# Value products in one piece and transposes two banks at a time, in a fused attention and two-layer MLP kernel

## Chip, cores and metric

The kernel runs on one core of a Trainium2 chip. The metric is the device time of one execution in microseconds (us); a median is taken over several executions.

## What is computed

The reference takes `q`, `k`, `v` of 4 batches, 8 heads, 576 positions and 64 dimensions. Attention is a sum of two parts: one over means of four neighbouring positions (144 by 144), repeated four times, and one over the seven positions nearest to each query. Its output, 2304 tokens by 512, goes through two MLPs.

```python
def _attn_ref(q, k, v):
    ...
    out_d = sm_attn(q_d, k_d, v_d)
    out_up = np.repeat(out_d, factor, axis=2)
    mask = np.abs(pos[:, None] - pos[None, :]) < factor
    ...
    out_local = np.matmul(attn, v)
    return (out_up + out_local).astype(np.float32)

def _moe_ref(x, w_in, w_out):
    h = x @ w_in
    g = h * (1.0 / (1.0 + np.exp(-1.702 * h)))
    return g @ w_out

def _moe2_ref(x, w1, w2, w3, w_out):
    return ((x @ w1) * (x @ w2) @ w3) @ w_out
```

## The kernel before, in words

The heads are worked on in 16 pairs (`HP` = 4 pairs for each of 4 batches), two heads side by side on the 128 partitions. TensorE is also given the MLPs: every large product is three matmuls of split operands (`mm3`, lines 117 to 120), the rows of L118, L119 and L120.

The program has these stages. First the product `w3 @ w_out2` is made (`w34_mm`, 192 large matmuls), and batch 0 of the attention is mixed into it. Then come five blocks of tokens of the first MLP (`h_step`, `y_step`); in block 0 batch 1 of the attention is mixed in, in block 1 batch 2, in block 2 batch 3. Blocks 3 and 4 and the second MLP (`ab_step`, `o_tile`) have no attention beside them.

The mixing is done by a list of pieces. `stage(n, what, own_exp)` returns the pieces of pair `n`: "T" transposes q and k (`t_piece`; by TensorE for batches 0 and 1 only, by VectorE for the others), "S" the scores (`s_local` twice, `s_pool`), "P" transposes the probabilities (`p_piece`, four transposes a bank), "V" the value products. `att_pieces` puts them into one list for a batch, in which `None` is an empty place, and `Pump` takes one place off the list after each group of three large matmuls (in the blocks after each second group). So a piece of the list is where its TensorE instructions are put among the large matmuls. A scheduler then orders all instructions by the priority that this program order gives and by when it takes them to be ready, so that a piece may come some places later than in the list, or next to another.

Before, "V" has three pieces: `v_pool` (line 404; four products with the pooled values into a PSUM bank `ps_vp`, copied by ScalarE to `od`, line 413), and `v_local` twice (line 415; ten and eight windows of 64 queries into a bank `ps_v`; VectorE adds `od` and writes `xo`, line 426, which SyncE's queue sends to `x_d`, line 430). Each product is recorded as two matmuls, so the rows show 8, 20 and 16. All of `ps_t`, `ps_s`, `ps_sp`, `ps_pt`, `ps_vp` and `ps_v` take turns in the two banks of the pool `pst`. For the four pairs of batch 3 (`LOCAL`) the near positions are not worked out by TensorE but by VectorE and GpSimd from about block 0 on (`l_scores`, `l_values`, the names `prod` and `ql`), and only the pooled part goes through "S", "P" and "V".

The first piece of "P" also calls `v_means` (line 298): GpSimd makes the pooled values `vd` from `s_v`, and ScalarE's queue then issues the load of the next pair's `s_v` (line 256), which has to wait until `vd` is made, as `s_v` has one buffer.

Of the kernel before, what the change touches and what calls it, by code (L numbers as in the profile page):

```python
# [8 lines left out]
F32 = mybir.dt.float32  # L9
# [11 lines left out]
def fused_kernel(ctx, tc, q, k, v, w_in, w_out1, w1, w2, w3, w_out2, out):  # L21
    nc = tc.nc
    B, H, S, D = q.shape
    FAC = 4
    SD = S // FAC
# [7 lines left out]
    HP = H // 2  # L33
    UC = SD // 2
    QB = 64
    NQB = S // QB
# [4 lines left out]
    HQ = (NQB + 1) // 2  # L41
# [3 lines left out]
    LOCAL = {12: 2, 13: 2, 14: 3, 15: 3}  # L45
# [9 lines left out]
    NB = 512  # L55
# [14 lines left out]
    g2p = ctx.enter_context(tc.tile_pool(name="g2p", bufs=2))  # L70
# [6 lines left out]
    pst = ctx.enter_context(tc.tile_pool(name="pst", bufs=2, space=PSUM))  # L77
# [149 lines left out]
    at = {}  # L227

    def head_ap(src, b, hp, tok, dims):
        off = ((b * H + 2 * hp) * S + tok) * D  # L230
        return bass.AP(src.tensor, src.offset + off, dims)
# [28 lines left out]
    def att_load_v(n):  # L260
        b, hp = divmod(n, HP)
        for t, i0, i1 in ((0, 0, HQ), (1, HQ, NQB)):
            vw = at["vw", n, t] = att.tile([KW, i1 - i0, 2, D], F32, tag=f"vw{t}", name="vw")
            for j0, j1 in ((i0, i0 + 1 - t), (i0 + 1 - t, i1 - t), (i1 - t, i1)):
                tok = min(max(j0 * QB - FAC, 0), S - KW)
                if j1 - j0 == 1:
                    nc.sync.dma_start(
                        out=vw[:, j0 - i0], in_=head_ap(v, b, hp, tok, [[D, KW], [S * D, 2], [1, D]]))
                elif j1 > j0:
                    for h in range(2):  # L270
                        nc.sync.dma_start(out=vw[:, j0 - i0:j1 - i0, h], in_=head_ap(
                            v, b, hp, h * S + tok, [[D, KW], [QB * D, j1 - j0], [1, D]]))

    def t_piece(n, name, c):
        if c == 0:
            at[name, n] = att.tile([128, SD, FAC], F32, tag=name + "T", name=name + "T")
        st, dst = at["s" + name, n], at[name, n]
        if n // HP >= PE_T:
            if c == 0:
                nc.vector.transpose(dst.rearrange("p u r -> p (u r)"), st.rearrange("p a b -> p (a b)"))  # L280
        else:
            ps = pst.tile([128, FAC, UC], F32, tag="t", name="ps_t")
            for r in range(FAC):
                nc.tensor.transpose(ps[:, r], st[:, c, r].rearrange("p h d -> p (h d)"), ident[:UC, :UC])
            nc.scalar.activation(dst[:, c * UC:(c + 1) * UC].rearrange("p u r -> p r u"), ps, AF.Copy)
        if c == 1:
            if name == "q":
                d = qd[:, :SD]
            else:
                d = at["kd", n] = att.tile([128, SD], F32, tag="kd", name="kd")  # L290
            if n // HP in QK_V:
                nc.vector.tensor_reduce(d, dst, op=ALU.add, axis=X)
            else:
                nc.gpsimd.tensor_tensor(d, dst[:, :, 0], dst[:, :, 1], op=ALU.add)
                for r in range(2, FAC):
                    nc.gpsimd.tensor_tensor(d, d, dst[:, :, r], op=ALU.add)
# [83 lines left out]
    NPT = NQB + 2 * NPB  # L380
    NPH = 8

    def p_piece(n, i0, i1):
        if i0 % NPH == 0 and i0 // NPH >= (n in LOCAL):
            at["PT", n, i0 // NPH] = att.tile(
                [KW, min(NPH, NPT - i0), 128], F32, tag=f"PT{i0 // NPH}", name="PT")
        i0 = i0 if n not in LOCAL else max(i0, NQB)
        ps = pst.tile([KW, i1 - i0, 128], F32, tag="t", name="ps_pt")
        for i in range(i0, i1):
            if i < NQB:  # L390
                src = at["el", n][:, i]
            else:
                kc, j = divmod(i - NQB, NPB)
                src = at["ep", n][:, j, kc * UC:(kc + 1) * UC]
            nc.tensor.transpose(ps[:, i - i0], src, ident)  # L395
        nc.scalar.activation(at["PT", n, i0 // NPH][:, i0 % NPH:i0 % NPH + i1 - i0], ps, AF.Copy)
        first = i0 == (0 if n not in LOCAL else NQB)
        if first:
            v_means(n)
            if n % HP < HP - 1 and n + 2 < B * HP:  # L400
                att_load(n + 2, "qk")

    def v_pool(n):
        PT, vd = at["PT", n, 1], at["vd", n]
        ps = pst.tile([128, SD], F32, tag="t", name="ps_vp")
        for kc in range(2):
            for h in range(2):
                p = slice(h * D, (h + 1) * D)
                i = NQB + kc * NPB - NPH
                nc.tensor.matmul(  # L410
                    ps[p], vd[:, h, kc], PT[:, i:i + NPB, h * QB:h * QB + PB], start=kc == 0, stop=kc == 1)
        at["od", n] = od = att.tile([128, SD], F32, tag="od", name="od")
        nc.scalar.activation(od, ps, AF.Copy, scale=1.0 / FAC)

    def v_local(n, i0, i1):
        vw, od = at["vw", n, i0 // HQ], at["od", n]
        xo = g2p.tile([128, NB], F32, tag="ys", name="xo")[:, :(i1 - i0) * QB]
        ps = pst.tile([128, (i1 - i0) * QB], F32, tag="t", name="ps_v")
        for i in range(i0, i1):
            for h in range(2):  # L420
                p = slice(h * D, (h + 1) * D)
                nc.tensor.matmul(
                    ps[p, (i - i0) * QB:(i - i0 + 1) * QB], vw[:, i - i0, h], at["PT", n, i // NPH][:, i % NPH, h * QB:(h + 1) * QB],
                    start=True, stop=True)
        u0, u1 = i0 * UB, i1 * UB
        nc.vector.tensor_tensor(
            xo.rearrange("p (u r) -> p u r", r=FAC), ps.rearrange("p (u r) -> p u r", r=FAC),
            od[:, u0:u1].unsqueeze(2).to_broadcast([128, u1 - u0, FAC]), op=ALU.add)
        b, hp = divmod(n, HP)
        nc.sync.dma_start(out=x_d[:, hp, b * S + i0 * QB:b * S + i1 * QB], in_=xo)  # L430
        if i1 == NQB and n + 1 < B * HP and n + 1 not in LOCAL:
            att_load_v(n + 1)


    def l_load(n):
# [57 lines left out]
    def l_out(n, i0, i1):  # L493

        o_d, od = at["od_", n], at["od", n]
        c0, c1 = i0 * QB // 32, i1 * QB // 32
        st = dp.tile([128, c1 - c0, 32], F32, tag="dec", name="ost")
        for i in range(4):
            h, dh = divmod(i, 2)
            nc.sync.dma_start(  # L500
                out=st[i * 32:(i + 1) * 32],
                in_=o_d[h, c0 * 32:c1 * 32, dh * 32:(dh + 1) * 32].rearrange("(c t) d -> t c d", t=32))
        xo = g2p.tile([128, NB], F32, tag="ys", name="xo")[:, :(i1 - i0) * QB]
        nc.vector.transpose(xo, st.rearrange("p c d -> p (c d)"))
        u0, u1 = i0 * UB, i1 * UB
        xv = xo.rearrange("p (u r) -> p u r", r=FAC)
        nc.vector.tensor_tensor(
            xv, xv, od[:, u0:u1].unsqueeze(2).to_broadcast([128, u1 - u0, FAC]), op=ALU.add)
        b, hp = divmod(n, HP)
        nc.sync.dma_start(out=x_d[:, hp, b * S + i0 * QB:b * S + i1 * QB], in_=xo)  # L510

    def stage(n, what, own_exp):
        if what == "T":
            return [lambda name=name, c=c: t_piece(n, name, c) for name in "qk" for c in range(2)]
        if n in LOCAL and what in "SPV":
            if what == "S":
                return [lambda: s_pool(n, False)]
            if what == "P":
                return [lambda: p_piece(n, NPH, NPH + 4), lambda: p_piece(n, NPH + 4, NPT)]
            return [lambda: v_pool(n), lambda: l_out(n, 0, HQ), lambda: l_out(n, HQ, NQB)]  # L520
        if what == "S":
            return [lambda: s_local(n, 0, HQ, own_exp), lambda: s_local(n, HQ, NQB, own_exp), lambda: s_pool(n, own_exp)]
        if what == "P":
            return [lambda i=i: p_piece(n, i, min(i + 4, NPT)) for i in range(0, NPT, 4)]
        return [lambda: v_pool(n), lambda: v_local(n, 0, HQ), lambda: v_local(n, HQ, NQB)]

    def att_pieces(b, own_exp, rest):

# [253 lines left out]
    if True:  # L782
# [72 lines left out]
        local, wait = local_pieces(), [0]  # L855
# [16 lines left out]
        for j in range(nblk):  # L872
# [14 lines left out]
            for f in range(NF):  # L887
# [6 lines left out]
                else:  # L894
# [8 lines left out]
                    if last and f >= NF2 + 2:  # L903
                        for _ in range(2):
                            if w34_raw:
                                fw, t = w34_raw.pop(0)
# [79 lines left out]
```

## Time and profile before

| | us |
|---|---|
| median of 3 runs | 899.37 |
| lowest and highest | 895.59, 905.09 |
| the profiled execution | 903.21 |
| its span on the core | 901.4 |
| mean granted clock of TensorE | 0.936 |

The span holds everything from the first instruction to the last; 1.8 us of the profiled execution lie outside it. A matmul's row ends only when its result is written, while the next one has long begun, so that what a matmul takes of TensorE's time is read from start to start.

### The profile page before, as it was taken

To read this page: it belongs to the slowest core of one execution; us is meant where nothing else is said; L and a number is where in the kernel's file an instruction comes from. 1 tells how busy PE (TensorE), PEld (TensorE's weight loads), DVE (VectorE), ACT (ScalarE), POOL (GpSimd) and SP (SyncE) were. 2 spreads that over 40 slices of the span, in tenths; PEclk is the share of its full clock that TensorE was granted. 3 is DMA by queue.
4 is the path that set the end of the run, shared out by engine and by line. 5 is a ranking of instruction groups with operands and counts; after the bars stand their busy time and mean duration, and the time that the engine had idled before them with its cause. 6 is when DMAs were issued, how large, how long until landed. Compare 5 with 4: busy or idle time off the path is not lost.

```text
span 901.4 us, 13594 instructions
## 1 busy us (share of the span) xinstructions
PE 849.8 (94%) x5132; PEld 712.6 (79%) x5132; DVE 605.9 (67%) x1061; ACT 384.2 (43%) x748; POOL 151.5 (17%) x153
## 2 busy tenths in 40 slices
PE   4788979989899999999999999999999999999998
PEld 3566767767677767767788988888999899989996
DVE  5997588879999999964448784342555554555551
ACT  4667567657654344344436554342212321131111
POOL 7535242134333332310100000000000000000000
PEclk9789888999999999989999999999999999999999
DMA  8875584555563344342357999201646364645521
GB/s 226 281 213 151 158 248 139 154 180 174 133 184 78 84 103 112 96 115 58 67 147 265 330 343 367 84 1 47 245 164 249 136 227 181 227 158 203 206 83 70
DMA packets 140598, 150.76 MB, mean 167 GB/s; under 512 B 86898, under 2 KB 121460, under 8 KB 136436
## 3 DMA queue, kind: packets, MB, share of 16 engines
q1 hardware_dynamic: 119424, 141.21, 48.3%
q10 hardware_dynamic: 21108, 8.69, 4.1%
q8 instruction: 40, 0.66, 0.3%
q14 instruction: 26, 0.21, 0.1%
HBM read 117.75 MB, written 32.11 MB: 166 GB/s over the span
## 4 chain that ended last, share of the span: by engine, by line
PE 69%; DVE 15%; DMA 5%; issue 4%; ACT 3%; POOL 3%; ACTq 0%; SPq 0%; DVEq 0%; POOLq 0%
PE ps_ab L120 6%; PE ps_ab L118 6%; PE ps_ab L119 6%; PE ps_h L118 5%; PE ps_y L118 5%; PE ps_h L119 5%; PE ps_h L120 5%; PE ps_y L120 5%; PE ps_y L119 5%; PE ps_o L119 4%; PE ps_o L120 4%; PE ps_o L118 4%; DVE dec L179 2%; PE ps_pt L395 2%; DVE st L176 2%
## 5 line engine op out<-in xcount | busy, mean ns | idle before, releaser
L118 PE MATMUL ps_h<-x_t,w 128*128 128x512 f32 (+1 forms) x320 | 123.3, 388 | 3.9 <-DVE w L115 2.9
L119 PE MATMUL ps_h<-x_t,w 128*128 128x512 f32 (+1 forms) x320 | 120.4, 376 | 4.1 <-DVE x_t L115 4.1
L118 PE MATMUL ps_y<-gh,w 128*128 128x512 f32 (+1 forms) x320 | 121.6, 381 | 0.0
L120 PE MATMUL ps_h<-x_t,w 128*128 128x512 f32 (+1 forms) x320 | 119.2, 373 | 0.0
L120 PE MATMUL ps_y<-gh,w 128*128 128x512 f32 (+1 forms) x320 | 118.8, 371 | 0.0
L119 PE MATMUL ps_y<-gl,w 128*128 128x512 f32 (+1 forms) x320 | 118.4, 370 | 0.4 <-DVE gl L115 0.4
L120 PE MATMUL ps_ab<-b_t,a_in 128*128 128x384 f32 x336 | 112.5, 335 | 0.0
L118 PE MATMUL ps_ab<-b_t,a_in 128*128 128x384 f32 x336 | 112.5, 335 | 0.0
L119 PE MATMUL ps_ab<-b_t,a_in 128*128 128x384 f32 x336 | 112.4, 334 | 0.0
L115 DVE TENSOR_TENSOR gl<-g_t,gh 128x512 fp32r<-128x512 f32 (+1 forms) x80 | 56.1, 704 | 69.8 <-ACT gh L114 68.8
L624 ACT ACTIVATE g_t<-ps_h 128x512 f32<-128x512 f32 (+1 forms) x80 | 44.0, 553 | 115.1 <-PE ps_h L120 111.5
L118 PEld LDWEIGHTS ps_h<-x_t,w 128*128 128x128 f32 x320 | 60.5, 191 | 18.6 <-DVE w L115 4.6
L119 PEld LDWEIGHTS ps_h<-x_t,w 128*128 128x128 f32 x320 | 61.1, 191 | 14.7 <-DVE x_t L115 5.7
L114 ACT ACTIVATE abh<-ab 128x384 fp32r<-128x384 f32 x24 | 12.6, 526 | 137.2 <-DVE ab L749 137.2
L118 PEld LDWEIGHTS ps_y<-gh,w 128*128 128x128 f32 x320 | 60.3, 189 | 11.8 <-issue 2.3
L120 PEld LDWEIGHTS ps_h<-x_t,w 128*128 128x128 f32 x320 | 61.1, 191 | 10.4 <-issue 0.2
L120 PEld LDWEIGHTS ps_y<-gh,w 128*128 128x128 f32 x320 | 60.4, 189 | 10.4
L119 PEld LDWEIGHTS ps_y<-gl,w 128*128 128x128 f32 x320 | 60.5, 189 | 9.5 <-DVE gl L115 1.0
L118 PEld LDWEIGHTS ps_ab<-b_t,a_in 128*128 128x128 f32 x336 | 63.1, 188 | 0.9
L119 PEld LDWEIGHTS ps_ab<-b_t,a_in 128*128 128x128 f32 x336 | 63.1, 188 | 0.9
L120 PEld LDWEIGHTS ps_ab<-b_t,a_in 128*128 128x128 f32 x336 | 63.1, 188 | 0.0
L179 DVE SCALAR_TENSOR_TENSOR dec<-dec,st 128x512 int32<-128x512 int32 x72 | 58.9, 828 | 5.6 <-ACT dec L166 4.7
(149 smaller groups left out, 1653.1 us busy)
## 6 DMA issues: line engine op xcount, KB each, us to landing
a_in<-a_d SPq DMA_DIRECT2D x24, 1792.0 KB
st<-in_moe_w_dram SPq DMA_DIRECT2D x32, 512.0 KB
a_d<-ap SPq DMA_DIRECT2D x8, 1792.0 KB
st<-in_moe_w_out_dram SPq DMA_DIRECT2D x24, 512.0 KB
st<-in_moe_w_in_dram SPq DMA_DIRECT2D x16, 512.0 KB
yr<-y_d SPq DMA_DIRECT2D x12, 384.0 KB
out_dram<-osb SPq DMA_DIRECT2D x17, 256.0 KB
s_v<-in_v_dram ACTq DMA_DIRECT2D x15, 288.0 KB
```

The costliest lines, as they stand in the source:

```text
L114: nc.scalar.activation(hi, raw, AF.Copy)
L115: lo_eng.tensor_tensor(lo, raw, f32(hi), op=ALU.subtract)
L118: nc.tensor.matmul(ps, ll, rh, start=start, stop=False, skip_group_check=more)
L119: nc.tensor.matmul(ps, lh, rl, start=False, stop=False, skip_group_check=more)
L120: nc.tensor.matmul(ps, lh, rh, start=False, stop=stop, skip_group_check=more)
L176: nc.vector.scalar_tensor_tensor(low, st[:, :, 1], -0x80000000, low, op0=ALU.bitwise_and, op1=ALU.bitwise_or)
L179: nc.vector.scalar_tensor_tensor(t, t, 3, st[:, :, 0], op0=ALU.logical_shift_left, op1=ALU.bitwise_or)
L395: nc.tensor.transpose(ps[:, i - i0], src, ident)
L624: nc.scalar.activation(g[:, :n], ps[:, :n], AF.Gelu_apprx_sigmoid)
```

## The change

"V" becomes one piece at the third of its three places. It takes both banks of `pst` at once: the first holds the pooled products and the last four windows, the second the first five. All TensorE instructions of the pair are written one after the other, then ScalarE's `od`, then VectorE's two `xo`. "T" writes the transposes of both banks of q (and of k) at the place of the second, and "P" those of two banks at the place of the second. The number of places in the list stays the same. No matmul, addition or transfer is added or left out. For batch 3 "V" stays in three pieces.

```diff
-    def v_pool(n):
+    def v_all(n):
+        both = pst.tile([128, NB], F32, tag="t", name="ps_v")
+        rest = pst.tile([128, NB], F32, tag="t", name="ps_v")
+        local = ((HQ, NQB, both[:, SD:SD + (NQB - HQ) * QB]), (0, HQ, rest[:, :HQ * QB]))
+        v_pool_mm(n, both[:, :SD])
+        for i0, i1, ps in local:
+            v_local_mm(n, i0, i1, ps)
+        v_pool(n, both[:, :SD])
+        for i0, i1, ps in local:
+            v_local(n, i0, i1, ps)
+        if n + 1 < B * HP and n + 1 not in LOCAL:
+            att_load_v(n + 1)
...
+        def together(*fns):
+            return [None] * (len(fns) - 1) + [lambda: [fn() for fn in fns]]
+
         if what == "T":
-            return [lambda name=name, c=c: t_piece(n, name, c) for name in "qk" for c in range(2)]
+            return [p for name in "qk" for p in together(*(
+                lambda name=name, c=c: t_piece(n, name, c) for c in range(2)))]
...
         if what == "P":
-            return [lambda i=i: p_piece(n, i, min(i + 4, NPT)) for i in range(0, NPT, 4)]
-        return [lambda: v_pool(n), lambda: v_local(n, 0, HQ), lambda: v_local(n, HQ, NQB)]
+            return [p for i in range(0, NPT, NPH) for p in together(*(
+                lambda i=i: p_piece(n, i, min(i + 4, NPT)) for i in range(i, min(i + NPH, NPT), 4)))]
+        return [None, None, lambda: v_all(n)]
```

**TensorE, the value products of the second pair of batch 2 in block 1.** Before, three groups stand apart (`ps_vp` is the pooled part, `ps_v` the windows, `ps_y` and `ps_h` the MLP):

```order
L410 MATMUL ps_vp<-PT,vd 64x144 x4
L118 MATMUL ps_y<-gh,w 128x512
L119 MATMUL ps_y<-gl,w 128x512
L120 MATMUL ps_y<-gh,w 128x512
...
L422 MATMUL ps_v<-PT,vw 64x64 x10
L118 MATMUL ps_h<-x_t,w 128x512
L119 MATMUL ps_h<-x_t,w 128x512
L120 MATMUL ps_h<-x_t,w 128x512
...
L422 MATMUL ps_v<-PT,vw 64x64 x8
```

In the changed kernel there:

```order
L118 MATMUL ps_h<-x_t,w 128x512
L119 MATMUL ps_h<-x_t,w 128x512
L120 MATMUL ps_h<-x_t,w 128x512
L428 MATMUL ps_v<-PT,vd 64x144 x4
L440 MATMUL ps_v<-PT,vw 64x64 x18
L118 MATMUL ps_h<-x_t,w 128x512
L119 MATMUL ps_h<-x_t,w 128x512
```

All 22 products stand in one row at the place of the last group. Over the 12 pairs of batches 0 to 2, the value products stand in 33 rows without a large matmul between them before, and in 18 now: six pairs in one, six in two. All small products together stand in 140 such rows before, in 111 now.

**ScalarE, the eviction of the pooled products of the second pair of batch 1.** Before (`od` is that eviction, `s_v` the load for the pair after next):

```order
L624 ACTIVATE g_t<-ps_h 128x512
L114 ACTIVATE gh<-g_t 128x512
L413 ACTIVATE od<-ps_vp 128x144
L256 DMA s_v<-in_v_dram 72x4x256
L364 ACT_TABLE_LOAD
```

In the changed kernel:

```order
L114 ACTIVATE w<-dec 128x512 x2
L256 DMA s_v<-in_v_dram 72x4x256
L433 ACTIVATE od<-ps_v 128x144
L366 ACT_TABLE_LOAD
```

The load now stands ahead of `od`; so it does for three of the 12 pairs. On VectorE the two additions of that pair, before and now:

```order
L426 TENSOR_TENSOR xo<-ps_v,od 128x320
L367 TENSOR_REDUCE sm<-ep 128x3
L176 SCALAR_TENSOR_TENSOR st<-st 128x512
...
L426 TENSOR_TENSOR xo<-ps_v,od 128x256
```

```order
L115 TENSOR_TENSOR w<-dec,w 128x512
L448 TENSOR_TENSOR xo<-ps_v,od 128x256
L448 TENSOR_TENSOR xo<-ps_v,od 128x320
L115 TENSOR_TENSOR gl<-g_t,gh 128x512
```

They stood nine rows apart, and now follow one another.

## Rows read from the trace of the kernel before

**Rows 1.** The page, busy time of each engine (share of the span) and instructions.

```profile
PE 849.8 (94%) x5132; PEld 712.6 (79%) x5132; DVE 605.9 (67%) x1061; ACT 384.2 (43%) x748; POOL 151.5 (17%) x153
```

**Rows 2.** Busy time in blocks 0 and 1: stretch, length, engines, clock, DMA share, GB/s.

```profile
198.50:400.00 201.50, 191.15 (x1321) 144.57 (x1320) 186.64 (x300) 100.30 (x162) 66.79 (x48) 0.94 0.48 125
```

**Rows 3.** Waits of TensorE, 56 to 400 us: total us, times, longest us.

```profile
PE ps_pt L395 <- POOL el L375: 5.2, 4, 2.5
...
PE ps_pt L395 <- ACT PT L396: 2.1, 2, 1.3
PE ps_t L284 <- DVE xo L426: 1.7, 1, 1.7
PE ps_v L422 <- ACT od L413: 1.6, 1, 1.6
```

**Rows 4.** Timeline of TensorE, one pair in block 0: start, us, row.

```profile
251.80 0.39 PE L120 MATMUL ps_y<-gh,w 128*128 128x512 f32 x1
252.12 0.72 PE L410 MATMUL ps_vp<-PT,vd 72*64 72x144 f32 x8
252.77 0.50 PE L118 MATMUL ps_y<-gh,w 128*128 128x512 f32 x1
253.10 0.40 PE L119 MATMUL ps_y<-gl,w 128*128 128x512 f32 x1
...
254.03 0.40 PE L120 MATMUL ps_y<-gh,w 128*128 128x512 f32 x1
254.36 1.27 PE L422 MATMUL ps_v<-PT,vw 72*64 72x64 f32 x36
255.56 0.50 PE L118 MATMUL ps_y<-gh,w 128*128 128x512 f32 x1
255.89 0.39 PE L119 MATMUL ps_y<-gl,w 128*128 128x512 f32 x1
```

**Rows 5.** Timeline of TensorE, ten windows alone.

```profile
107.29 0.39 PE L118 MATMUL ps_w<-w,w3t 128*128 128x512 f32 x1
107.61 0.80 PE L422 MATMUL ps_v<-PT,vw 72*64 72x64 f32 x20
108.34 0.50 PE L119 MATMUL ps_w<-w,w3t 128*128 128x512 f32 x1
108.68 0.39 PE L120 MATMUL ps_w<-w,w3t 128*128 128x512 f32 x1
```

**Rows 6.** Timeline of TensorE, pooled products and ten windows without a gap.

```profile
115.91 0.40 PE L119 MATMUL ps_w<-w,w3t 128*128 128x512 f32 x1
116.24 0.73 PE L410 MATMUL ps_vp<-PT,vd 72*64 72x144 f32 x8
116.80 0.75 PE L422 MATMUL ps_v<-PT,vw 72*64 72x64 f32 x20
117.48 0.49 PE L120 MATMUL ps_w<-w,w3t 128*128 128x512 f32 x1
117.91 0.69 PE L422 MATMUL ps_v<-PT,vw 72*64 72x64 f32 x16
```

**Rows 7.** Timeline of TensorE, the end of a bank of transposes of probabilities.

```profile
316.55 0.50 PE L395 MATMUL ps_pt<-ident,ep 128*72 128x128 f32 x3
316.80 0.48 PE L118 MATMUL ps_y<-gh,w 128*128 128x512 f32 x1
317.12 0.40 PE L119 MATMUL ps_y<-gl,w 128*128 128x512 f32 x1
317.35 0.40 PE L120 MATMUL ps_y<-gh,w 128*128 128x512 f32 x1
```

**Rows 8.** Timeline of ScalarE, at the second and the third pair of batch 1.

```profile
207.90 0.29 ACT L413 ACTIVATE od<-ps_vp 128x144 f32<-128x144 f32 x1
...
209.05 1.28 ACT L364 ACT_TABLE_LOAD   x1 [0.85 <-POOL vd L303]
...
237.64 1.28 ACT L364 ACT_TABLE_LOAD   x1 [3.35 <-POOL vd L303]
```

More of the change, by code (lines that the diff above doesn't have):

```diff
@@ L401, in p_piece, with v_far, v_pool_mm @@
                 att_load(n + 2, "qk")
-    def v_pool(n):
+    def v_all(n):
[10 more added lines that the diff above has]
+            att_load_v(n + 1)
+    def v_far(n):
+        ps = pst.tile([128, SD], F32, tag="t", name="ps_vp")
+        v_pool_mm(n, ps)
+        v_pool(n, ps)
+    def v_pool_mm(n, ps):
         PT, vd = at["PT", n, 1], at["vd", n]
-        ps = pst.tile([128, SD], F32, tag="t", name="ps_vp")
         for kc in range(2):
@@ L411, in v_pool, with v_local_mm @@
                     ps[p], vd[:, h, kc], PT[:, i:i + NPB, h * QB:h * QB + PB], start=kc == 0, stop=kc == 1)
+    def v_pool(n, ps):
         at["od", n] = od = att.tile([128, SD], F32, tag="od", name="od")
         nc.scalar.activation(od, ps, AF.Copy, scale=1.0 / FAC)
[L415 to L418, printed above, removed]
+    def v_local_mm(n, i0, i1, ps):
+        vw = at["vw", n, i0 // HQ]
         for i in range(i0, i1):
@@ L424, in v_local @@
                     start=True, stop=True)
+    def v_local(n, i0, i1, ps):
+        od = at["od", n]
+        xo = g2p.tile([128, NB], F32, tag="ys", name="xo")[:, :(i1 - i0) * QB]
         u0, u1 = i0 * UB, i1 * UB
@@ L430, in v_local @@
         nc.sync.dma_start(out=x_d[:, hp, b * S + i0 * QB:b * S + i1 * QB], in_=xo)
-        if i1 == NQB and n + 1 < B * HP and n + 1 not in LOCAL:
-            att_load_v(n + 1)
     def l_load(n):
@@ L518, in stage @@
             if what == "P":
-                return [lambda: p_piece(n, NPH, NPH + 4), lambda: p_piece(n, NPH + 4, NPT)]
-            return [lambda: v_pool(n), lambda: l_out(n, 0, HQ), lambda: l_out(n, HQ, NQB)]
+                return together(lambda: p_piece(n, NPH, NPH + 4), lambda: p_piece(n, NPH + 4, NPT))
+            return [lambda: v_far(n), lambda: l_out(n, 0, HQ), lambda: l_out(n, HQ, NQB)]
         if what == "S":
```

## The prediction

> **What bounds the kernel now.** I read the page's busy times first. TensorE is busy for 849.8 us, 94% of the span, VectorE for 67%, ScalarE for 43% [rows 1]. So the kernel is a stream of matmuls, and what takes TensorE less time, at a place where TensorE sets the pace, comes off the end. Second is the stretch from 198.5 to 400 us, where batches 1 and 2 of the attention are mixed into blocks 0 and 1 and where two thirds of the changed value products stand. There TensorE is busy for 191.15 of 201.5 us, but VectorE for 186.64, which leaves it 14.9 us of idle time [rows 2]. TensorE is still ahead as the bound, by little: what stops VectorE there is soon felt. Third are TensorE's own waits from 56 to 400 us. Four of them are at pieces that the change touches: transposes that wait for GpSimd's normalised `el` (5.2 us in 4), transposes that wait for a bank which ScalarE empties (2.1 us in 2), one that waits for a bank which VectorE's `xo` empties (1.7), and windows that wait for a bank until `od` is copied (1.6) [rows 3]. Last is TensorE's timeline, from start to start, for what one piece among the large matmuls costs.
>
> **What a piece costs.** A large matmul starts 0.23 us after the one before it (317.12 to 317.35 [rows 7]). A piece's cost is the time from the start of the large matmul ahead of it to that of the second one behind it, less two such steps, 0.46. Four pooled products alone: 251.80 to 253.10 is 1.30, so 0.84 us. All 18 windows in one: 254.03 to 255.89 is 1.86, so 1.40 [rows 4]. Ten windows alone: 107.29 to 108.68 is 1.39, so 0.93 [rows 5]. Ten windows are 20 recorded matmuls, 18 are 36: the 16 more cost 0.47, or 0.029 each, so that 20 of them are 0.59 and 0.34 us are a fixed price of the piece. It can be seen where it is paid: the first value product starts 0.32 to 0.33 us after the large matmul instead of 0.23, and the second large matmul behind a piece starts 0.33 to 0.34 after the first; the rest lies inside the piece. By this eight windows alone are 0.34 + 16 x 0.029 = 0.81. A check of the fixed price with the other kind: pooled products with ten windows behind them. From 115.91 to 117.91 is 2.00, less 0.46, less 0.10, as the next step leads into another value piece, gives 1.44; apart they are 0.84 + 0.93 = 1.77, so 0.33 less [rows 6]. So a pair in three pieces costs 0.84 + 0.93 + 0.81 = 2.58 us, in one 1.90, and each join is worth 0.34.
>
> **The change part by part.**
>
> Value products. The twelve pairs of batches 0 to 2 have them in 33 rows before and in 18 now, as the order of instructions shows: 15 joins x 0.34 = 5.1 us less of TensorE's time. No product goes away, so this is all there is on the engine itself.
>
> Transposes. Behind a bank of them the second large matmul starts 0.32 us after the first (316.80 to 317.12), 0.09 over the usual step [rows 7], and that is the most that a join can save. The order has some 12 such joins more, two banks of q, k or probabilities side by side: between 0 and 1.1 us. I take 0.3, near the lower end, as two banks side by side still start their own matmuls one by one. The score products stand in one row more than before, which I price like a value piece: 0.34 lost. These two cancel.
>
> The Trainium skill ("TensorEngine Tiling (Array Packing)", section "Key Properties") says that changing the tiling mode, not just the tile, drains TensorE. By that alone a join of value products (64 columns wide, between matmuls 128 wide) saves the drains, as the rows above show at both ends of a piece, while two banks of transposes in the large matmuls' own mode save nothing; the sum would then be 5.1 less 0.34, and by the 0.09 us up to 5.9.
>
> The banks. The value products now hold both banks of `pst` at once, and the next piece that wants one waits for `od` (0.29 us, the row at 207.90 [rows 8]) and one or two `xo`. Before, a bank could come free between the pieces; but then the second windows could be held up by `od` themselves, the 1.6 us of rows 3, and that wait has no place any more. Two empty places stand ahead of each joined piece, six or twelve large matmuls (1.4 or 2.8 us at 0.23), time for the banks to be emptied. A new wait is bounded by the old ones of its kind, 0 to 1.7 us each [rows 3]; I take none over the 1.6 that goes and count both as nothing.
>
> `od` on ScalarE. For three of the 12 pairs the load of `s_v` now stands ahead of `od` in ScalarE's queue, and waits until GpSimd has made `vd`, which itself waits for the pooled products. Until now only what stood behind `od` waited so: an exponential's table load for 0.85 us at the second pair of batch 1, and for 3.35 at the third [rows 8]. Now `od` does, and behind it both `xo`, which follow one another on VectorE, and behind these all that VectorE has to do, among it the `gl` of the MLP. Price: 3 x 0.85 to 3 x 3.35, or 2.6 to 10.1 us of VectorE's time; I take the lower, since the row of one of these very pairs has 0.85. With 14.9 us idle on VectorE [rows 2], it costs the end nothing.
>
> Sum: 5.1 us less. On the profiled execution, 903.21 us with its 901.4 us span and 1.8 us around it, that gives 898.1. That execution lies 3.8 above the median of 899.37, and the same difference off the median is 894.3.
>
> **The rivals.**
>
> *Nothing is gained.* The joined products come earlier only for TensorE to wait longer at the next piece, since GpSimd and VectorE don't get faster; VectorE at 186.64 of 201.5 us speaks for it [rows 2], against it that the waits in this whole stretch are few and that between them TensorE runs without a gap. Then the time stays at 899.
>
> *VectorE stands at the additions.* Both `xo` now follow directly on `od`, with no piece of TensorE's between, so every pair makes VectorE wait for at least the copy: 9 x 0.29 = 2.6, and 3 x 3.35 = 10.1 for those behind the load, 12.7 us in all. It decides from where these stalls no longer fall into VectorE's idle time, 14.9 us over the whole stretch but not at these places. If none of it is covered, the end moves by 12.7 - 5.1 = +7.6: 907, slower than before. For it: how full VectorE is [rows 2], and the 3.35 us [rows 8]; against it: `gl` is needed only two steps later by TensorE, some 24 large matmuls or 5.5 us. The Trainium skill ("PSUM — Partial Sum Buffer", section "Engine vs sequencer instructions") has the queues of ScalarE and VectorE as strict FIFO, and this rival lives by that; the 3.35 us of rows 8 agree, an exponential that stood behind a load it had no need of.
>
> *The waits go as well.* With both banks claimed at once and the first half of P a place later, the waits for banks (2.1 + 1.7 + 1.6 = 5.4 us) and half of those for `el` (2.6) go too [rows 3]: 5.1 + 5.4 + 2.6 = 13.1 less, 886. Against it: the joined piece needs two free banks instead of one.
>
> That the change doesn't do what it says holds for six pairs, whose ten windows still stand apart from the rest in the order; the 15 joins already count that, and it is no rival of its own.
>
> **How the numbers follow.** My forecast, 894.3, gets 0.45; nothing gained, 899, 0.20; VectorE at the additions, 907, 0.15; the waits go too, 886, 0.20. The range runs from 885, just past the fast rival, to 907, the slow one. A measurement can tell this kernel from no change at about 1%, 9 us: under 890.4 is faster, over 908.4 slower. Faster: most of the fast rival and a tail of the forecast, 0.25. Slower: the part of the slow rival where more than its 12.7 us are felt, and tails, 0.11. Within 1%: 0.64.
>
> **What would show it.** Right: TensorE's starts show a pair's 22 products in 2.36 us from the large matmul ahead to the second behind (1.90 + 0.46), there are six such rows and six pairs in two, and TensorE's busy time falls by some 5 us with the waits as they were. The slow rival shows as VectorE idle before `xo` with `od` as the releaser, and as `gl` among TensorE's waits; the one without gain as longer waits of the transposes for `el`; the fast one as rows 3 without its lines on `PT`, `xo` and `od`. I am wrong on the mechanism if a joined piece still costs as much as its parts, 2.58 us.

## The result and the profile after

| | before | after |
|---|---|---|
| median, us | 898.64 (20 runs) | 904.81 (20 runs) |
| lowest, highest | 892.90, 905.09 | 901.26, 910.16 |
| ratio to before | 1 | 1.0063 [1.0044, 1.0082] |
| profiled execution, span | 903.21, 901.4 | 904.45, 902.7 |
| mean granted clock over the runs | .9843 (30 runs beside the first experiments) | .9758 |

The change costs 6 us where 5 were forecast as saved. The page's busy line of the changed kernel, beside [rows 1]:

```profile
PE 850.9 (94%) x5132; PEld 721.8 (80%) x5132; DVE 607.2 (67%) x1061; ACT 387.5 (43%) x750; POOL 149.5 (17%) x153
```

TensorE's busy time should have fallen by 5 us and rose by 1.1. Yet the pieces cost what was worked out. TensorE's timeline at a joined pair of the changed kernel (start, us, row):

```profile
240.01 0.39 PE L120 MATMUL ps_y<-gh,w 128*128 128x512 f32 x1
240.33 0.71 PE L428 MATMUL ps_v<-PT,vd 72*64 72x144 f32 x8
240.87 1.22 PE L440 MATMUL ps_v<-PT,vw 72*64 72x64 f32 x36
242.02 0.50 PE L118 MATMUL ps_y<-gh,w 128*128 128x512 f32 x1
242.36 0.39 PE L119 MATMUL ps_y<-gl,w 128*128 128x512 f32 x1
```

From 240.01 to 242.36 is 2.35 us, as forecast (2.36). Now TensorE's waits from 56 to 400 us, beside [rows 3]:

```profile
PE ps_sp L352 <- DVE el L336: 6.3, 2, 4.0
PE ps_h L119 <- DVE x_t L115: 3.7, 3, 1.9
PE ps_h L118 <- ACT x_t L114: 2.8, 2, 1.5
PE ps_h L118 <- DVE w L115: 2.5, 1, 2.5
...
PE ps_pt L395 <- POOL el L375: 1.4, 2, 1.0
...
PE ps_pt L395 <- ACT PT L396: 0.4, 2, 0.3
PE ps_pt L395 <- DVE xo L448: 0.4, 2, 0.2
```

The four lines of [rows 3], 10.6 us, are down to 2.2: that is what the fast rival asked for. But a line that was not among them now leads, 6.3 us for `el`, the step in which VectorE empties the banks of local scores (L336). Before, that line was:

```profile
PE ps_sp L352 <- DVE el L336: 1.0, 1, 1.0
```

All waits of TensorE in this stretch come to 24.2 us before and to 26.3 after. VectorE at the longer of the two waits for `el`, and TensorE's rows, its local scores and the pooled ones that were held up:

```profile
197.99 0.43 DVE L173 TENSOR_SCALAR st<-st 128x512 int32<-128x512 int32 x1 [3.79 <-DMA st<-in_moe_w_out_dram]
198.45 0.69 DVE L176 SCALAR_TENSOR_TENSOR st<-st 128x512 int32<-128x512 int32 x1
201.01 0.43 DVE L173 TENSOR_SCALAR st<-st 128x512 int32<-128x512 int32 x1 [1.86 <-DMA st<-in_moe_w_in_dram]
201.47 0.69 DVE L176 SCALAR_TENSOR_TENSOR st<-st 128x512 int32<-128x512 int32 x1
202.08 0.69 DVE L115 TENSOR_TENSOR gl<-g_t,gh 128x512 fp32r<-128x512 f32 x1
202.68 0.53 DVE L336 TENSOR_TENSOR el<-ps_s,band 128x360 f32<-128x360 f32 x1
```

```profile
196.98 0.85 PE L333 MATMUL ps_s<-kT,qT 64*64 64x72 f32 x20
203.36 1.70 PE L352 MATMUL ps_sp<-kd,qd 64*64 64x144 f32 x12 [4.01 <-DVE el L336]
```

In VectorE's queue `el` stood behind two weight decodes (L173), and these waited until their loads had landed, 3.79 and 1.86 us. The scores were ready and not emptied; so TensorE had no bank for the pooled scores. Before, the same step stood ahead of these two decodes:

```profile
200.07 0.85 PE L333 MATMUL ps_s<-kT,qT 64*64 64x72 f32 x20
201.04 0.53 DVE L336 TENSOR_TENSOR el<-ps_s,band 128x360 f32<-128x360 f32 x1
202.69 0.43 DVE L173 TENSOR_SCALAR st<-st 128x512 int32<-128x512 int32 x1
202.60 0.97 PE L352 MATMUL ps_sp<-kd,qd 64*64 64x144 f32 x12
```

So TensorE came to these scores 3.1 us earlier than before, and they were emptied 1.6 us later. This wait is not the whole loss, as the versions with one part of the change show: those with only the value products, or only batch 0's, wait 0.4 us and not at all for this `el` from 56 to 400 us, and are slow too (below). Last the granted clock, in four stretches of block 0 (columns: stretch, length, busy PE, PEld, DVE, ACT, POOL with counts, PEclk, DMA share, GB/s). Before:

```profile
125.00:140.00 15.00, 10.90 (x83) 8.67 (x82) 11.03 (x20) 10.04 (x18) 6.29 (x7) 0.74 0.70 221
165.00:169.00 4.00, 4.00 (x36) 3.05 (x35) 2.60 (x5) 2.89 (x7) 0.00 (x0) 0.95 0.49 81
200.00:206.00 6.00, 6.00 (x63) 4.53 (x63) 5.50 (x11) 4.78 (x10) 0.00 (x0) 0.95 0.59 180
230.00:238.00 8.00, 8.00 (x69) 5.93 (x68) 7.40 (x15) 2.52 (x5) 3.23 (x1) 0.95 0.59 127
```

After:

```profile
125.00:140.00 15.00, 12.09 (x76) 9.64 (x73) 9.33 (x18) 7.56 (x14) 3.99 (x6) 0.56 0.78 228
165.00:169.00 4.00, 3.83 (x32) 2.69 (x33) 2.54 (x5) 3.69 (x7) 0.00 (x0) 0.57 0.35 113
200.00:206.00 6.00, 2.64 (x14) 2.10 (x15) 4.96 (x10) 2.16 (x4) 0.00 (x0) 0.76 0.02 6
230.00:238.00 8.00, 5.70 (x27) 4.22 (x26) 6.33 (x13) 1.70 (x2) 0.00 (x0) 0.79 0.56 142
```

The full level is recorded as 0.95 in the one profile and 1.00 in the other, though a large matmul's step is 0.23 us in both; so it is the falls below it that count. Each is a stretch at the lower level, 1.2 GHz, where the step is 0.43 us, and each comes with a wait of TensorE. Before has 27 us of them within its span, after 51.

**A balance used below.** For each profile I split the span into TensorE's idle time (the sum of the gaps ahead of its rows), the price of the lower level (half of the time at that level outside gaps) and the rest, TensorE's own work at full speed. Before: 47.9 + 12.0 + 841.5 = 901.4. After: 48.0 + 21.9 + 832.7 = 902.7 (the parts are rounded). In these two profiles, then, TensorE's work did fall, by 8.8 us, and the lower level took 9.9 back. Two cautions go with every use of this balance. Each profile is one execution. And that of before is a slow one of its kernel, 4.6 us over the median of 898.64, so that the two spans differ by 1.3 us only where the medians differ by 6.2: the other 4.9 us are in executions that left no trace.

### The profile page after: what moved, and what is told of

Read it like the earlier page. It is cut to its first block, busy times and chain, and to the rows that moved or that the text cites. A ratio compares the mean times of both kernels' runs of the same rounds, so it can differ in the third digit from the quotient of the medians.

```text
span 902.7 us, 13607 instructions
## 1 busy us (share of the span) xinstructions
PE 850.9 (94%) x5132; PEld 721.8 (80%) x5132; DVE 607.2 (67%) x1061; ACT 387.5 (43%) x750; POOL 149.5 (17%) x153
## 4 chain that ended last, share of the span: by engine, by line
PE 71%; DVE 15%; DMA 6%; issue 4%; ACT 3%; POOL 2%; ACTq 0%; SPq 0%; DVEq 0%; POOLq 0%
PE ps_ab L120 6%; PE ps_ab L118 6%; PE ps_ab L119 6%; PE ps_h L119 5%; PE ps_h L118 5%; PE ps_h L120 5%; PE ps_y L118 5%; PE ps_y L120 5%; PE ps_y L119 5%; PE ps_o L119 4%; PE ps_o L120 4%; PE ps_o L118 4%; DVE dec L179 2%; DMA st<-in_moe_w_in_dram 2%; DVE st L176 2%
## 5 line engine op out<-in xcount | busy, mean ns | idle before, releaser
L118 PE MATMUL ps_h<-x_t,w 128*128 128x512 f32 (+1 forms) x320 | 123.2, 386 | 5.3 <-ACT x_t L114 2.8
L119 PE MATMUL ps_h<-x_t,w 128*128 128x512 f32 (+1 forms) x320 | 122.9, 385 | 4.0 <-DVE x_t L115 3.9
L120 PE MATMUL ps_h<-x_t,w 128*128 128x512 f32 (+1 forms) x320 | 120.9, 378 | 0.0
L118 PEld LDWEIGHTS ps_h<-x_t,w 128*128 128x128 f32 x320 | 62.0, 194 | 17.9 <-ACT x_t L114 3.7
L119 PEld LDWEIGHTS ps_h<-x_t,w 128*128 128x128 f32 x320 | 62.3, 195 | 15.8 <-DVE x_t L115 5.7
L120 PEld LDWEIGHTS ps_h<-x_t,w 128*128 128x128 f32 x320 | 62.5, 195 | 10.6 <-issue 0.2
L179 DVE SCALAR_TENSOR_TENSOR dec<-dec,st 128x512 int32<-128x512 int32 x72 | 58.9, 830 | 5.1 <-ACT dec L166 3.8
```

What stands on the lines that cost most here:

```text
L118: nc.tensor.matmul(ps, ll, rh, start=start, stop=False, skip_group_check=more)
L119: nc.tensor.matmul(ps, lh, rl, start=False, stop=False, skip_group_check=more)
L120: nc.tensor.matmul(ps, lh, rh, start=False, stop=stop, skip_group_check=more)
L179: nc.vector.scalar_tensor_tensor(t, t, 3, st[:, :, 0], op0=ALU.logical_shift_left, op1=ALU.bitwise_or)
```

## Experiments

### Which part loses

Four kernels with one part of the change each; the others are written as before. In `stage`, for example:

```diff
-            return [p for name in "qk" for p in together(*(
-                lambda name=name, c=c: t_piece(n, name, c) for c in range(2)))]
+            return [lambda name=name, c=c: t_piece(n, name, c) for name in "qk" for c in range(2)]
...
-        return [None, None, lambda: v_all(n)]
+        return [None, None, lambda: v_all(n)] if n < HP else [
+            lambda: v_pool0(n), lambda: v_local0(n, 0, HQ), lambda: v_local0(n, HQ, NQB)]
```

`v_pool0` and `v_local0` are the functions of the kernel before.

> Only the value products are joined (12 pairs); transposes stay in two pieces. The changed kernel took 904.8 us against 898.6. Theory A, low clock: the joined products save their 5 us of TensorE time, but waits in blocks 0 and 1 fall so that TensorE's granted clock drops to half more often; the time follows the length of the low-clock stretches (before 27 us of them, after 51 us; each us costs about half a us). Then any variant is at 898.6 minus its joins x 0.34 us plus half of its extra low-clock time: for this one 894 with as much low clock as before, up to 905 with that of the changed kernel. Theory B, block 0 is paced by the loads of its weights: what is saved ahead of its end comes back as waits, only batch 2 counts: 897 to 899. Theory C, the transposes are to blame (P's first bank one place later moves the loads of q, k and v onto those of the weights): this one is faster by its 14 joins, 894, and e2_transposes slower, about 909.

> Only the transposes of q, k and probabilities are joined two banks at a time; value products stay in three pieces. A: about 898 with as much low clock as before, and half a us more for each us of low clock over 27. B: 898 to 899, no difference. C: slower, about 909.

> Value products joined for the 4 pairs of batch 0 only (beside the product of the weights, ahead of block 0). A: 3 joins, 897.6 plus half of any extra low clock. B: TensorE reaches block 0 earlier (the changed kernel: 3.6 us) and waits there for weights just as much longer: 898.6, and TensorE's lead is lost by the end of block 0. C: 897.6.

> Value products joined for the 8 pairs of batches 1 and 2 only. A: some 11 joins, 895 plus half of any extra low clock. B: only batch 2's joins count, some 6 x 0.34: 896.6. C: 895.

| | median, us | ratio to before | mean clock |
|---|---|---|---|
| only value products joined | 902.20 | 1.0032 [1.0007, 1.0058] | .9773 |
| only transposes joined | 903.37 | 1.0057 [1.0027, 1.0088] | .9820 |
| value products of batch 0 only | 903.75 | 1.0066 [1.0035, 1.0097] | .9783 |
| value products of batches 1 and 2 only | 901.78 | 1.0034 [1.0004, 1.0064] | .9828 |

Every part alone costs 3 to 5 us, down to the third, which joins only batch 0's products. The parts do not add up to the whole, so it is not one of them. The theory that one kind of piece loses (C) falls, and so does the one by which the weight loads hold every version to the same end (B). The lower clock (A) is only half borne out. With the 41, 24, 41 and 41 us at the lower level that the four profiles show, its rule gives 900.8, 896.5, 904.6 and 902.0: within 1.5 us three times, and 7 us too low for the transposes, which lose without more of the lower level in their profile; by the mean clock of all their runs 3 us are still missing. By the balance the value products alone take 6.6 us off TensorE's work and the transposes nothing, as forecast for these.

### Filling the waits

Matmuls whose result is overwritten, at three of the waits that both kernels share:

```diff
+    FILL = {("w", 0, 4): 4, ("w", 0, 6): 3, ("s", HP): 2}
...
+    def keep_busy(ps, n):
+        for _ in range(n):
+            nc.tensor.matmul(ps, ident, band.rearrange("p a b -> p (a b)"), start=True, stop=True)
...
         ps = psh.tile([128, 4, 128], F32, tag="h", name="ps_w")
+        keep_busy(ps.rearrange("p a b -> p (a b)")[:, :432], FILL.get(("w", half, j), 0))
```

> The kernel before, with nine matmuls whose result is thrown away, put where TensorE waits longest early in the program: four of 128x432 ahead of the fifth w3 transposition (in the trace of before it waits 3.87 us at 39.69), three ahead of the seventh (2.27 us at 53.04), two ahead of the pooled scores of batch 1's first pair (3.65 us at 132.56). The rest of TensorE's order stays as it was but for some 37 of 4540 places. Theory D (what a wait costs is above all the half-speed stretch behind it): the stretches at the 1.2 GHz level at 39.4, 53.1 and 131.6 us, 13.6 us of before's 27.7, shrink to under 7; the mean granted clock over the runs rises from .985 to .990 or more; although work is added the time falls to 893 to 897. Rival E (the clock is a bystander; a wait costs its length): nine matmuls of about 0.75 us fill about 6.7 of 9.8 us of waits and change nothing, 898 to 901.

> The changed kernel with the same nine matmuls at the same three places (its waits there: 3.91 us at 39.69, 2.32 at 53.09, 2.15 at 129.28). Theory D: the half-speed stretches at 39.3 (6.8 us), 53.0 (3.4) and 124.6 (13.7), together 23.9 of its 53 us, fall to about 10; mean clock from .9755 to .982 or more, time from 904.8 to 896 to 900. Rival E: 904 to 908 at a clock that stays near .976. If it comes out level with the kernel before (898.6) or under it, the saving in TensorE's work is seen to be real and the clock to have hidden it.

Before with it: 900.10, ratio 1.0012 [0.9983, 1.0041], mean clock .9883. After with it: 905.82, 1.0071 [1.0043, 1.0100], .9859. The clock rose, in the kernel before not quite to theory D's .990, in the changed kernel past that of before, and the time did not move. In the first of them (windows, columns as above):

```profile
39.00:60.00 21.00, 17.01 (x114) 12.69 (x114) 20.51 (x30) 9.01 (x17) 9.63 (x9) 0.92 0.63 185
...
127.00:140.00 13.00, 12.10 (x88) 8.73 (x89) 10.79 (x19) 8.92 (x16) 4.84 (x6) 1.00 0.76 253
```

From 39 to 60 us VectorE is busy for 20.51 of 21.00. That points to its decoding as what sets when this stretch ends; then the speed at which TensorE waits for it has no price. From 127 to 140 the clock now stays at its full level. The balance of this one profile, against that of before, is idle -8.3, lower level -2.8, work +7.6 us: what was filled in took the place of what it was meant to save. In the changed kernel the lower level falls by 7.9 and the work grows by 9.4; the idle time did not even fall (50.5 us for 48.0), because other waits grew, one of 5.3 us for `gl` among them. So D's forecast failed in both kernels: the spare matmuls take the sign of a wait away and not the wait. What a higher clock would be worth without added work, this pair cannot show.

### Taking the new wait away

```diff
-        nc.vector.tensor_tensor(e[:, i0:i1], ps, band[:, b0:b0 + i1 - i0], op=ALU.min)
+        with tc.high_priority(150):
+            nc.vector.tensor_tensor(e[:, i0:i1], ps, band[:, b0:b0 + i1 - i0], op=ALU.min)
```

> The changed kernel with VectorE's emptying of the local score banks given a higher priority than the decoding of weights, so that it stands a few rows further ahead in VectorE's queue (in the changed kernel it stood behind decodes that waited 3.79 and 1.86 us for their weights, and TensorE waited 4.01 us at 203.4 and 2.3 at 233.8 for it). Theory F (the loss is these new waits in block 0 and the half-speed stretches behind them): both waits under 1 us, TensorE's waits for el (line 336 of before) from 6.6 to under 3 us, the stretches at 203 and 234 gone, 899 to 902. Rival (they only move to the next wait): idle sum as before, 904 to 906.

910.33, ratio 1.0122 [1.0093, 1.0152]: a miss of both forecasts, and the slowest of all kernels with joined pieces. TensorE at the same place:

```profile
203.82 1.37 PE L353 MATMUL ps_sp<-kd,qd 64*64 64x144 f32 x12 [4.14 <-DVE el L337]
```

The wait is the same as before the edit: `el` again came behind two decodes that waited 4.02 and 1.76 us for their loads. The edit did not bring about what it was to test, so it says nothing for or against theory F.

### Another order of the same pieces

All pieces of batch 1 one place later, nothing else:

```diff
-        n0, out_ = b * HP, []
+        n0, out_ = b * HP, [None] * (1 if b == 1 else 0)
```

> The kernel before with all pieces of batch 1 called one place later, nothing joined: the same instructions, 132 in place of 133 insertions between large matmuls, 397 of TensorE's 4540 places moved. Theory G (the order of before is a lucky one, and any other order of the same pieces meets more waits and more half-speed stretches): slower by 0.2 to 0.7%, 900.5 to 905, at a mean clock of .983 or under. Rival H (the loss belongs to joined pieces, and an order without them is as good): within 0.2%, 897 to 900.5, clock near .985.

903.73, ratio 1.0032 [1.0008, 1.0056], mean clock .9824: without a single joined piece, about as slow as the parts of the change. This is theory G's result.

### Is VectorE or are the loads the pace

The decoding of block 0's weights without the operation that puts a weight's sign back, and, as a version that does all the work, a split moved to GpSimd:

```diff
-            for st, t in sts:
+            for st, t in sts if early["sign"] else ():
...
-            jobs.append((("wo1", f), lambda f=f: load_rows(w_out1, f), nc.vector, f < 3))
+            jobs.append((("wo1", f), lambda f=f: load_rows(w_out1, f), nc.vector if f < 3 else nc.gpsimd, f < 3))
```

> The kernel before without one VectorE operation of the weight decoding in block 0 (the one that puts a weight's sign back: 28 of 0.70 us in its trace between 117 and 262 us, 19.7 us of VectorE's 122.6 busy there). It leaves the signs of those weights out; TensorE's work, the loads and ScalarE's work stay. Theory V (TensorE and VectorE are both nearly full here, 126.5 and 122.6 us of 140.3, and VectorE with its waits for weights sets when block 0 ends): 892 to 896, block 0 shorter by 4 to 8 us. Rival B (the weight loads set it): within 2 us of 899, VectorE only waits longer for its loads. Rival P (TensorE and its order set it): within 2 us of 899.

> The changed kernel without the same VectorE operation in block 0. Theory V: here TensorE has less to do, so it gains more than the kernel before from a lighter VectorE: 891 to 897, by 8 us or more under the changed kernel's 904.8, and level with or under the run of the kernel before without that operation. Rival B (loads): 902 to 906. Rival P (order and half-speed stretches): 902 to 906, and the two trimmed kernels stand as far apart as the untrimmed, some 6 us.

> The kernel before with the second half of the weight split for w_out1 (13 of 16 tiles) on GpSimd in place of VectorE: some 13 times 0.7 = 9 us off VectorE in block 0, 13 times 1.26 = 16 us more on GpSimd, which is busy for 47 of block 0's 140 us. All work is done. Theory V: 2 to 4 us faster, 895 to 897. Rivals B and P: within 1 us of 899, or slower where a matmul now waits for GpSimd.

> The changed kernel with the same split on GpSimd. Theory V: 4 to 7 us faster than the changed kernel, 898 to 901. Rivals B and P: 903 to 907.

With the lighter decoding: before 901.23, ratio 1.0010 [0.9983, 1.0036], after 898.58, 0.9988 [0.9962, 1.0013]. VectorE's waits for weights between 117 and 262 us in the lighter kernel before (us, times, longest):

```profile
DVE st L173 <- DMA st<-in_moe_w_out_dram: 8.6, 5, 4.0
DVE st L173 <- DMA st<-in_moe_w_in_dram: 8.0, 7, 1.9
```

They were 3.1 and 5.9 in the kernel before. VectorE has less to do there and waits 7.6 us longer for its loads, as rival B said, and nothing is gained, as B and P both had it. The changed kernel gained 6.2 us by the same edit, though there too VectorE waits 5.1 us longer for these loads (19.9 for 14.8): less than theory V's 8, more than B or P allow. Whether it gained by the lighter engine or by the new order, this pair cannot tell. With the split on GpSimd both lost: 913.58, 1.0147 [1.0113, 1.0182], and 909.46, 1.0101 [1.0066, 1.0136]. VectorE's idle time ahead of L179, waiting for ScalarE's `dec`, was 2.0 us before and is 8.9 in the first of these:

```profile
L179 DVE SCALAR_TENSOR_TENSOR dec<-dec,st 128x512 int32<-128x512 int32 x28 | 23.4, 848 | 8.9 <-ACT dec L166 8.7
```

Two other operations of the decoding also take longer there than before, L176 778 ns for 707 and L173 638 for 501. Theory V falls here. B and P allowed for a loss if a matmul had to wait for GpSimd's split, but none of TensorE's seven largest waits is one for it; why it loses 1.5%, some 13 us, was not followed further. In both couples the changed kernel is now ahead, with the lighter decoding by less than the runs can tell.

### Each shift with and without the change

The shift of batch 1 by one place in the changed kernel too; by two places in both kernels; that of batches 1 to 3 by one place in both; and by two places in the changed one.

> The changed kernel with all pieces of batch 1 called one place later: the same work, 447 of TensorE's 4540 places moved. Its partner without the change is the kernel before with the same shift, 903.73. Theory G (the order of the pieces scatters the time by some 4 us to either side, before's own order is among the good ones, and TensorE's saving is there beneath it): 896 to 902, under its partner's 903.7. Rival H (joined pieces lose by themselves): 906 to 911, over its partner by the 6 us that the change cost in the unshifted pair.

> The changed kernel with all pieces of batch 1 called two places later (571 of 4540 places moved). Theory G: anywhere between 895 and 905, on average over the three shifts 2 to 5 us under the kernel before with the same shift. Rival H: 4 to 8 us over it.

> The kernel before with all pieces of batch 1 called two places later, nothing joined (484 of 4540 places moved). Theory G: 899 to 907, nearer to 903.7 (the shift by one) than to 898.6. Rival H (orders without joined pieces are as good as before's): 897.5 to 900.5.

> The changed kernel with all pieces of batches 1, 2 and 3 called one place later (802 of 4540 places moved). Theory G: 895 to 905, on average over the three shifts 2 to 5 us under its partner. Rival H: 4 to 8 us over its partner.

> The kernel before with all pieces of batches 1, 2 and 3 called one place later, nothing joined (878 of 4540 places moved): the partner of the shifted changed kernel that came out at 895.43. Theory G (order scatters, TensorE's saving of 5.1 us lies beneath): 898 to 905, 3 to 9 us over its partner. Rival H (the shift is what gained, and joined pieces lose): 889 to 893, under its partner.

> The changed kernel with all pieces of batches 1, 2 and 3 called two places later. Theory G: somewhere from 895 to 907, as the five orders of the joined pieces so far (895.4 to 906.7); no rule that the run could give says which. Rival (later pieces are better by themselves): under 895.4.

All couples, as medians and ratios to the kernel before in runs beside them, and what the balance of the two profiles says (with the change less without it, us). The kernel before itself had medians from 898.4 to 900.5 in these sets of runs, so the difference is that of the ratios.

| both kernels with | without | with the change | difference | work | idle | lower level |
|---|---|---|---|---|---|---|
| nothing else | 898.64 | 904.81, 1.0063 | +0.63% | -8.8 | +0.1 | +9.9 |
| batch 1 one later | 903.73, 1.0032 | 901.01, 1.0018 | -0.14% | -4.7 | +2.4 | -0.6 |
| batch 1 two later | 900.41, 1.0014 | 906.67, 1.0064 | +0.50% | -5.8 | +8.0 | +9.4 |
| batches 1 to 3 one later | 904.29, 1.0043 | 895.43, 0.9956 | -0.87% | -7.1 | -4.1 | +3.7 |
| nine spare matmuls | 900.10, 1.0012 | 905.82, 1.0071 | +0.59% | -7.0 | +10.9 | +4.8 |
| lighter decoding | 901.23, 1.0010 | 898.58, 0.9988 | -0.22% | -9.1 | +3.7 | +5.0 |
| a split on GpSimd | 913.58, 1.0147 | 909.46, 1.0101 | -0.46% | -6.9 | +1.6 | +2.5 |
| batches 1 to 3 two later | not tried | 896.64, 0.9949 | | | | |

Rival H falls: the change does not lose by itself. It is ahead in four couples of seven, clearly in two of these (-0.87% and -0.46%); its three losses are clear too. Theory G's own figures were met in part: over the three shifts the change is ahead by 0.17% or 1.5 us, where G had 2 to 5, one version lies over its range (906.67, for 895 to 905), and the shift by two places without the change is nearer to no shift than G had it. With the work left alone (the first four rows and the last), four orders without joined pieces lie between 898.6 and 904.3, five with them between 895.4 and 906.7. The order alone, then, is worth as much as the change was to bring, to either side. TensorE's work falls in every couple, by 7.0 us on average (standard error 0.6); the price of the lower level grows by 5.0 on average (1.4), in six of seven; the idle time by 3.2 (1.9), also in six of seven, which single profiles do not settle. For the clock all runs can be asked: its mean over a kernel's runs is lower with the change in six couples and level in the seventh (batches 1 to 3), by 0.0041 on average, or 3.7 us of 900. The mean of the seven differences in time is 0.00% with a standard error of 0.22 from their scatter of 0.58, so that 95% reach 0.54 to either side. A steady gain of 5.1 us, 0.57%, lies just outside that; whether there is a smaller one stays open, as does what makes one order good.

Two versions beat both kernels: the joined pieces with batches 1 to 3 one place later, 0.9956 [0.9934, 0.9979], and two places later, 0.9949 [0.9921, 0.9977]. They are the best of five orders, and were not known to be so beforehand. That later pieces are better by themselves they do not show: without joined pieces every shift was slower or level. The first one's busy line, and its largest waits from 56 to 400 us:

```profile
PE 844.6 (95%) x5132; PEld 717.7 (80%) x5132; DVE 604.8 (68%) x1061; ACT 389.8 (44%) x752; POOL 148.1 (17%) x153
```

```profile
PE ps_h L118 <- ACT x_t L114: 4.0, 3, 1.8
PE ps_h L118 <- DVE w L115: 3.6, 2, 3.0
PE ps_pt L395 <- POOL el L375: 2.6, 2, 1.8
...
PE ps_sp L352 <- DVE el L336: 0.7, 1, 0.7
```

Here TensorE is busy for 5.2 us less than in [rows 1], and the wait for `el` is 0.7 us where the changed kernel had 6.3.

## Why the prediction was wrong

*The pieces: right.* A joined pair is 2.35 us from the large matmul ahead to the second behind, forecast 2.36. Six pairs stand so and six in two pieces; where no other small product stands among these, they cost 1.31 + 0.93 = 2.24, forecast 2.58 - 0.34. TensorE's work fell by more than the 5.1 us of the sum, 7.0 on average; where the rest comes from was not followed.

*Transposes, the banks:* the waits for `PT`, `xo` and `od` went down with `el` of L375 from 10.6 to 2.2 us, more than the forecast took. That a new wait for a bank is bounded by the old ones of its kind, 1.7 us, was wrong: the pooled scores waited 4.0 for one. Only waits behind `od` and `xo` had been looked at, not what else stands ahead of the emptying of a bank on VectorE.

*`od` on ScalarE: right in kind.* ScalarE's timeline:

```profile
209.67 0.29 ACT L433 ACTIVATE od<-ps_v 128x144 f32<-128x144 f32 x1 [2.59 <-POOL vd L303]
```

It waits where the forecast had it, for 2.59 us, and 7.8 us in all over three waits, nearer to the upper end of the 2.6 to 10.1 than to the lower that was taken. VectorE has other work meanwhile: in block 0 its `xo` wait for `od` 0.2 us in all. The rival on VectorE's additions had the sign and not the mechanism.

*The step that failed* is the first, that what takes TensorE less time at a place where it sets the pace comes off the end, with a sum made of the changed pieces alone and all else standing still. TensorE's idle time was counted as unchanged, and its clock had no term at all, nor a reason for leaving it out. In the pair that was forecast the two profiles show work -8.8 us, idle time +0.1 and lower clock +9.9, where the sum had -5.1 and nothing; over the seven couples it is -7.0, +3.2 and +5.0. Nor did all else stand still: by the order of instructions 766 of TensorE's 4540 places hold something else than before. In blocks 0 and 1 TensorE was busy for 191.15 of 201.5 us and VectorE for 186.64 [rows 2]; after, it reads:

```profile
198.50:400.00 201.50, 185.19 (x1264) 144.65 (x1261) 183.20 (x293) 97.61 (x155) 63.30 (x48) 0.96 0.47 121
```

That neither sets the pace alone is the reading that fits: between the two stand queues in order, loads of weights, and two banks, and at the scores of 196.98 us a TensorE that was done sooner only waited sooner. The rival "nothing is gained" has the time of the average over orders, and it was given 0.20 and no scatter. Its mechanism is not confirmed: its sign, longer waits of the transposes for `el` (L375), did not come, as these fell from 5.2 to 1.4 us. In the single pair that was forecast, the order before was the fastest of its four (one of the others is within the uncertainty), and the one after the fourth of its five. So the 6 us of this pair are a matter of the two orders that were built; why one order is better than another is shown in part only, and the cause of that stays open.

## What to carry to other kernels

Where a scheduler orders the instructions, a saving of half a per cent can't be judged by one build: make a few neutral shifts of both versions, compare them in couples, and keep the best order. An engine that is 95% busy beside one that is 93% busy is not yet the pace; ask what it would wait for if it came sooner. A fall in the granted clock says where waits are; here, filling three of them with useless work raised the clock and returned no time.

## What the runs showed of the hardware

- Time and mean clock go together from run to run of one and the same kernel: of 30 runs of before, 17 at a mean clock of .985 or over took 897.3 us on average, 12 between .980 and .985 took 901.6; in four other sets of its runs the same split is worth 1.4 to 4.8 us. It does not follow that the clock is the cause: with the spare matmuls, which also add work, it was .9883 and the time 900.1.
- Short waits are enough for a long stretch at the lower level. From 122 to 129 us the changed kernel waits 0.92, 0.52 and 2.15 us between small products, and its clock is at the lower level for 13.7 us from 124.6 on.
- Moving 13 splits from VectorE, where one takes 0.80 us on average, to GpSimd, where it takes 1.61 and which is idle two thirds of that time, cost 1.5%, some 13 us.
